# The second batch's attention in float32, with transposes on TensorE and the division after the product

## The chip, the core and the metric

The kernel runs on one core of a Trainium2 chip. The metric is the time on the device of one execution, in microseconds, and lower is better. A core has five engines that each take their instructions in a fixed order: TensorE (PE, products; its weight loads are listed as PEld), VectorE (DVE), ScalarE (ACT), GpSimd (POOL) and SyncE (SP, which here only issues DMAs). Work is handed between them by semaphores. Products are written to PSUM, which has eight banks; everything else lives in SBUF.

## The reference

Attention with a sliding window of 128 and a linear bias over 8 batches, 8 heads, 576 positions and 64 channels, and then a bilinear feed-forward layer over the joined heads:

```python
scores = np.matmul(q, k.transpose(0, 1, 3, 2)) / np.sqrt(D)
mask = (rel >= 0) & (rel < 128)
scores = np.where(mask, scores + bias[None], -1000000000.0)
attn = np.exp(scores - np.max(scores, axis=-1, keepdims=True))
attn = attn / (np.sum(attn, axis=-1, keepdims=True) + 1e-09)
x = np.matmul(attn, v)                 # joined to (B * S, H * D)
out = ((x @ w_a) * (x @ w_b)) @ w_out  # 512 -> 1536 -> 512
```

## The kernel before

The work of a batch is attention for four pairs of heads, then an up projection (twelve blocks `f` of 128 hidden rows, for `w_a` and `w_b`), the product of the two halves, and a down projection. Batches follow each other, and attention of batch b + 1 is woven into the projections of batch b, in sevenths of a pair (`yield i + k / 7`). Float32 precision in the projections comes from splitting each operand into a float16 high and low part and adding three products.

The first batch has no projections to hide behind. Its attention (`first_attention`, L524) works in float32: scores (L569), exponentials without a division (L581), transposes as products with an identity on TensorE (L587), copies of these from PSUM (L592 to L595), the product with v (L501), and then a product of x with the reciprocals of the sums (L619), which an outer product has spread over the channels first (L603 to L614). Beside it run the first steps of `weights`, which loads the projection matrices, converts them from 64-bit words and splits them (L126 to L232). The rest of these steps runs along the first batch's up and down projections (`first_batch`, L999).

All later batches take their attention from `attention` (L658). It already gives the second batch (`o.b == 1`) float32 scores (L374), but then treats it as the others: exponentials (L383), division (`normalize`, L387: the reciprocals, then a float16 high part on ScalarE, L399, and the rest on VectorE, L400, both into the tile `phl`), a DMA transpose of `phl` into `pT` (L405), a split of v into high and low (`split_v`, L291), 42 float16 products a pair (`pv`, L503) and a copy of x (L414).

The first batch's up projection (`first_up`, L776) makes 576 products in groups of twelve, one PSUM bank each. Five banks (three `ef`, two `ch`, by `bank`, L59) go round in turn. A group for `w_a` is read by ScalarE (L783), a group for `w_b` by VectorE (L785), which multiplies the two; a bank is free again when it has been read. The down projection (`first_down`, L804) follows. In this part only SyncE's order is written by hand; a scheduler sets the order on the other engines. From the second batch's projections on, TensorE's order is that of the code.

Of the kernel before, what the change touches and what calls it, by code (L numbers as in the profile page):

```python
# [23 lines left out]
P = 128  # L24
# [5 lines left out]
VCOLS = 640  # L30
# [16 lines left out]
def attention_then_bilinear_ffn(ctx: ExitStack, tc: tile.TileContext, qT, kT, vP, w_a, w_b, w_out, rel, slopes2, outT):  # L47
# [42 lines left out]
    ratio = const.tile([P, NF], F32, name="ratio")  # L90
    smin = const.tile([P, 1], F32, name="smin")
    so = const.tile([P, 1], F32, name="so")

# [110 lines left out]
    def down_weights():  # L204

        sums = small.tile([P, NF // 2], F32, tag="wos", name="wos", bufs=1)
        for n in range(NF // 2 + 1):
# [12 lines left out]
        vec.reciprocal(sab, sab)  # L220
        s1 = small.tile([P, 1], F32, tag="wo1", name="wo1", bufs=1)
        vec.tensor_reduce(out=s1, in_=sums, op=ALU.add, axis=AX)
        tot = ps_at.tile([P, 512], F32, tag="at", name="wtot")
# [134 lines left out]
    def before_scores(o, ninv):  # L358
        o.bias = work.tile([P, WIN], F32, tag="bias", name="bias")
        last_bias[0] = pool.tensor_scalar(out=o.bias, in0=rel_sb, scalar1=ninv, scalar2=sl2_sb[:, o.p:o.p + 1], op0=ALU.mult, op1=ALU.mult)  # L360
        o.mn, o.sm, o.rin = (small.tile([P, 9], F32, tag=tag, name=tag) for tag in ("mn", "sm", "rin"))
        o.n, o.parts = 0, []

    def scores(o, bi):

        ps = ps_at.tile([P, 512], F32, tag="at", name="sc_ps")
        t = work.tile([P, 512], F32, tag="t", name="t", bufs=4)
        for i, c in BANKS[bi]:
# [10 lines left out]
        for i, c in BANKS[bi]:  # L379
            pc, w = TILES[i]  # L380
            n = o.n
            vec.tensor_tensor_reduce(out=t[:, c:c + w], in0=ps[:, c:c + w], in1=o.bias[:, WIN - w:WIN], scale=-0.125 if o.b == 1 else o.neg, scalar=3.0e38, op0=ALU.add, op1=ALU.min, accum_out=o.mn[:, n:n + 1])  # L382
            act.activation(t[:, c:c + w], t[:, c:c + w], AF.Exp, bias=o.mn[:, n:n + 1], scale=-1.0, accum_out=o.sm[:, n:n + 1])  # L383
            o.parts.append((n, t[:, c:c + w], pc, w))
            o.n += 1

    def normalize(o):  # L387

        a, z = o.parts[0][0], o.n

        if o.b < 2:
            vec.tensor_scalar(out=o.rin[:, a:z], in0=o.sm[:, a:z], scalar1=1e-9, scalar2=1.0 / PSC, op0=ALU.add, op1=ALU.mult)
        else:

            act.activation(o.rin[:, a:z], o.sm[:, a:z], AF.Copy, scale=1.0 / PSC, bias=1e-9 / PSC)
        vec.reciprocal(o.rin[:, a:z], o.rin[:, a:z])
        for m, e, pc, w in o.parts:
            s = o.rin[:, m:m + 1]
            act.activation(phl[:, 0, pc:pc + w], e, AF.Copy, scale=s)  # L399
            vec.scalar_tensor_tensor(out=phl[:, 1, pc:pc + w], in0=e, scalar=s, in1=phl[:, 0, pc:pc + w], op0=ALU.mult, op1=ALU.subtract)  # L400
        o.parts = []
# [256 lines left out]
    def attention():  # L658
# [28 lines left out]
        load(0)  # L687
        st, prev = load_v(1), None
        o = squares(0)
        lay_out(o)  # L690
        load(1)
        yield 0
        for i in range(n + 1):
            b, p = 1 + i // NPAIR, i % NPAIR

            two = 2 if o and o.b >= 2 else 1
            for bi in range(two if o else 0):
# [11 lines left out]
            if p == 2:  # L709
# [3 lines left out]
            elif prev and p != 1:  # L713
                prev.vhl = split_v(st, prev.p)
            yield i + 2 / 7
            if p == 2:
                pv(late.p, st, late, late.vhl)
                transpose_probs(prev)
                split(nxt)
            if o and p != 2:  # L720
                with behind():
                    normalize(o)
            if p != 2:
                split(nxt)
            yield i + 3 / 7
            if o:
                scores(o, 2)
            if prev and p not in (1, 2):
                pv(prev.p, st, prev, prev.vhl)
# [5 lines left out]
            yield i + 4 / 7  # L735
            if p == 2:
                prev.vhl = split_v(st, prev.p)
# [6 lines left out]
            load(i + 2)  # L744
            if p == 1:
                v_squares(st, (0, 1))
# [6 lines left out]
            if o:  # L753
                with behind():
                    normalize(o)
            if p == 1:
# [4 lines left out]
            if p == 2:  # L761
                pv(prev.p, st, prev, prev.vhl)
            if p == 1:
                late = prev
# [4 lines left out]

    states, started, first_reads, last_read, last_main, last_bias = {}, {"down": -1}, [None], [None], [None], [None]  # L770


# [202 lines left out]
    first = stack.enter_context(tc.tile_pool(name="first", bufs=1))  # L975
    ident = first.tile([P, P], F32, name="ident")
    make_identity(nc, ident)

# [80 lines left out]
```

## Time and profile before

| | us |
|---|---|
| median of 3 runs | 1007.48 |
| lowest and highest run | 1007.32, 1007.81 |
| span of the profiled execution | 1005.2 |
| first up-projection product of the second batch | 215.10 |

The span goes from the first to the last instruction of one profiled execution. For that execution the profile states the span alone; the median of the runs is 2.3 us above it, and so the time of the profiled execution is taken as its span and those 2.3 us. In the profile a line gives an engine, an operation, and the tiles written and read (out<-in). "Busy" is the time in which an engine executes, and an idle time is put down to what ended it. A float32 product leaves two records in the trace, a transpose one.

### The profile page before, as it was taken

The numbers are of one execution on the slowest core, as the hardware profiler recorded it, in microseconds if no ns is written. First come the engines' busy times: TensorE is split into PE (matmuls) and PEld (weight loads), VectorE is DVE, ScalarE is ACT, GpSimd is POOL, SyncE is SP. The second block draws the span as 40 slices with busy tenths as digits, with TensorE's granted clock in tenths as the row PEclk, the third lists the DMA queues.
The fourth block names the chain that finished last, engine by engine and source line by source line (L and its number), as shares of the span: only waits on it lengthen the run. The fifth ranks groups of instructions, "written<-read, shape, count | busy, mean of one in ns | idle before, by whom it ended". The sixth has DMA issues, their size and how long they took to land.

```text
span 1005.2 us, 23888 instructions
## 1 busy us (share of the span) xinstructions
PE 970.8 (97%) x9339; PEld 753.6 (75%) x9339; DVE 674.8 (67%) x1833; ACT 648.9 (65%) x1715; POOL 306.1 (30%) x345
## 2 busy tenths in 40 slices
PE   8789989999999999999999999999999999999998
PEld 5557656777777777777787777777777777777776
DVE  5888999557878566785768687666677576524530
ACT  7976779657767756767767767677666766413321
POOL 3533463104565321352226112220223022211100
PEclk9889999999999999999999999999999999999999
DMA  9317733564444442462624642474425632210001
GB/s 349 120 43 269 231 114 74 120 166 80 100 90 100 137 90 43 97 172 71 121 52 105 172 90 46 93 178 103 84 57 107 163 67 43 49 37 7 2 13 36
DMA packets 148433, 102.83 MB, mean 102 GB/s; under 512 B 120032, under 2 KB 128352, under 8 KB 147296
## 3 DMA queue, kind: packets, MB, share of 16 engines
q1 hardware_dynamic: 138816, 91.77, 37.2%
q10 hardware_dynamic: 9504, 9.54, 2.9%
q8 instruction: 73, 1.20, 0.5%
q14 instruction: 40, 0.33, 0.1%
HBM read 48.33 MB, written 9.44 MB: 57 GB/s over the span
## 4 chain that ended last, share of the span: by engine, by line
PE 70%; DVE 10%; ACT 4%; DMA 2%; issue 1%; POOL 1%; SPq 0%; ACTq 0%; DVEq 0%
PE dn_ps L932 19%; PE ch L836 19%; PE p L836 14%; PE up_ps L836 10%; PE x_ps L501 4%; PE sc_ps L378 3%; DVE phl L400 2%; PE dn_ps L812 2%; DMA v<-in_vP 1%; DVE t L382 1%; DVE xs L436 1%; ACT t L383 1%; DVE wup L150 1%; ACT phl L399 1%; DVE wup L257 1%
## 5 line engine op out<-in xcount | busy, mean ns | idle before, releaser
L836 PEld LDWEIGHTS <-wup 128*128 128x128 f16 x4224 | 409.1, 98 | 120.8 <-issue 14.3
L932 PE MATMUL dn_ps<-h,wdn 128*128 128x288 f16 x2016 | 254.3, 286 | 0.0
L932 PEld LDWEIGHTS <-wdn 128*128 128x128 f16 x2016 | 193.9, 98 | 51.7
L836 PE MATMUL ch<-xs,wup 128*128 128x288 f16 x1536 | 221.5, 286 | 0.8 <-ACT rc L861 0.6
L836 PE MATMUL up_ps<-xs,wup 128*128 128x288 f16 x1536 | 197.7, 288 | 5.8 <-DVE rc L785 4.2
L836 PE MATMUL p<-xs,wup 128*128 128x288 f16 x1152 | 172.6, 286 | 0.0
L891 POOL TENSOR_TENSOR rc<-rc,row 128x288 f32<-128x288 f32 x64 | 62.3, 974 | 278.8 <-DVE row L889 262.9
L400 DVE SCALAR_TENSOR_TENSOR phl<-t,rin,phl 128x192 f16<-128x192 f32 (+2 forms) x252 | 109.5, 474 | 19.0 <-ACT phl L399 18.8
L383 ACT ACTIVATE t<-t,mn 128x192 f32<-128x192 f32 (+2 forms) x252 | 107.2, 427 | 23.3 <-DVE mn L382 23.0
L829 ACT CAST h<-rc 128x576 f16<-128x576 f32 x96 | 64.2, 669 | 68.2 <-DVE rc L896 37.6
L399 ACT ACTIVATE phl<-t,rin 128x192 f16<-128x192 f32 (+2 forms) x252 | 88.7, 425 | 23.0 <-DMA pT<-phl 10.9
L830 DVE TENSOR_TENSOR h<-rc,h 128x576 f16<-128x576 f32 x90 | 71.1, 790 | 32.7 <-ACT h L829 32.0
L382 DVE CUSTOM_DVE_ANT_0 t<-sc_ps,bias,neg 128x192 f32<-128x192 f32 (+2 forms) x216 | 73.7, 389 | 7.8 <-PE sc_ps L378 7.7
L135 POOL TENSOR_TENSOR wup<-wup,wdn 128x512 int32<-128x512 int32 x36 | 54.6, 1539 | 44.6 <-DVE wup L133 14.6
L937 ACT ACTIVATE row<-dn_ps,oi 128x288 f32<-128x288 f32 x56 | 27.6, 494 | 56.7 <-PE dn_ps L932 56.5
L873 ACT ACTIVATE row<-ch,g 128x288 f32<-128x288 f32 x64 | 31.8, 497 | 50.1 <-PE ch L836 50.1
L436 DVE TENSOR_TENSOR xs<-v,xs 128x576 f16<-128x576 f32 x52 | 48.7, 950 | 21.7 <-ACT xs L435 21.5
L360 POOL TENSOR_SCALAR bias<-rel_sb,ninv,sl_sb 128x192 f32<-128x192 f32 x24 | 21.3, 887 | 123.5 <-DVE mn L382 123.5
L868 DVE TENSOR_TENSOR rc<-p,rc 128x288 f32<-128x288 f32 x64 | 29.1, 454 | 44.4 <-PE p L836 35.0
L896 DVE SCALAR_TENSOR_TENSOR rc<-rc,g,ch 128x288 f32<-128x288 f32 x64 | 32.6, 510 | 23.8 <-PE ch L836 23.6
L383 ACT ACTIVATION_READ_ACCUMULATOR t<-t,mn 128x1 f32 x252 | 47.7, 189 | 0.0
L430 POOL TENSOR_TENSOR xq<-xq,sq 128x576 bf16<-128x576 bf16 x22 | 29.6, 1345 | 56.8 <-ACT sq L429 56.7
(151 smaller groups left out, 1315.6 us busy)
## 6 DMA issues: line engine op xcount, KB each, us to landing
v<-in_vP SPq DMA_DIRECT2D x8, 1280.0 KB, 6.5
out<-row ACTq DMA_DIRECT2D x60, 144.0 KB, 1.8
qk<-in_qT SPq DMA_DIRECT2D x28, 288.0 KB, 3.9
qk<-in_kT SPq DMA_DIRECT2D x28, 288.0 KB, 4.4
wdn<-in_w_a SPq DMA_DIRECT2D x12, 512.0 KB, 4.5
wdn<-in_w_b SPq DMA_DIRECT2D x12, 512.0 KB, 5.6
wdn<-in_w_out SPq DMA_DIRECT2D x12, 512.0 KB, 4.3
qst<-qkh SPq DMA_DIRECT2D x24, 144.0 KB, 2.7
```

Of the source, the lines that this page charges most:

```text
L135: pool.tensor_tensor(out=t[:, m, :], in0=t[:, m, :], in1=low[:, m, :], op=ALU.add)
L382: vec.tensor_tensor_reduce(out=t[:, c:c + w], in0=ps[:, c:c + w], in1=o.bias[:, WIN - w:WIN], scale=-0.125 if o.b == 1 else o.neg, scalar= ...
L383: act.activation(t[:, c:c + w], t[:, c:c + w], AF.Exp, bias=o.mn[:, n:n + 1], scale=-1.0, accum_out=o.sm[:, n:n + 1])
L399: act.activation(phl[:, 0, pc:pc + w], e, AF.Copy, scale=s)
L400: vec.scalar_tensor_tensor(out=phl[:, 1, pc:pc + w], in0=e, scalar=s, in1=phl[:, 0, pc:pc + w], op0=ALU.mult, op1=ALU.subtract)
L436: vec.tensor_tensor(out=xs[:, n, 1, :, :], in0=src, in1=xs[:, n, 0, :, :], op=ALU.subtract)
L501: pe.matmul(xp[oc // 512][64 * h:64 * h + 64, o0:o0 + w], vt[0:rows, c:c + 64], probs(pt, rows, blocks, h), start=(n == 0 and first), stop ...
L829: act.copy(h[:, f, :, 0, :], hid)
L830: eng.tensor_tensor(out=h[:, f, :, 1, :], in0=hid, in1=h[:, f, :, 0, :], op=ALU.subtract)
L836: pe.matmul(ps[:, 0:HT], wup[:, a[0], a[1], wi, k, :], xs[:, b, xi, k, :], start=(first and n == 0), stop=(last and n == len(ks) - 1), ski ...
L891: pool.tensor_tensor(out=x0, in0=x0, in1=mid, op=ALU.mult)
L932: pe.matmul(ps[:, 0:HT], wdn[:, f, wi, e * P:(e + 1) * P], h[:, f, t, hi, :], start=(m == 0 and n == 0), stop=(m == NF - 1 and n == 2))
```

## The change

The second batch takes the first batch's way. Its exponentials stay undivided in four fixed buffers (`plain_ts`), zeroed once where the window leaves gaps. They are transposed on TensorE with the identity, copied from PSUM into a float32 tile (`phl` for even pairs, `pT` for odd ones), multiplied with v in float32, and x is multiplied with the spread reciprocals and v's scale on VectorE (`plain_pv`, which runs one pair behind in four steps). The splits of v and of the probabilities, the DMA transposes and the copy of x fall away for this batch. v's sums of squares and scale move to an earlier place; `phl` is zeroed when the third batch begins instead of before the projections. The identity stays allocated, and a few small tiles are merged.

```diff
+    two_scales = const.tile([P, 2], F32, name="two_scales")
+    smin, so = two_scales[:, 0:1], two_scales[:, 1:2]
+    ident = const.tile([P, P], F32, name="ident")
+    make_identity(nc, ident)
...
     def before_scores(o, ninv):
...
+        if o.b == 1:
+            o.pT = (new_pT().rearrange("p a c -> p (a c)") if o.p % 2 else phl.rearrange("p a c -> p (a c)")).bitcast(F32).rearrange("p (b q) -> p b q", q=P)
...
-        t = work.tile([P, 512], F32, tag="t", name="t", bufs=4)
+        t = plain_ts[bi] if o.b == 1 else work.tile([P, 512], F32, tag="t", name="t", bufs=4)
...
-            o.parts.append((n, t[:, c:c + w], pc, w))
+            o.parts.append((n, t[:, c:c + w], pc, w) if o.b > 1 else (bi, t))
...
+    def transpose_plain(o):
+        for bi, t in dict(o.parts).items():
+            tp = bank("tr_ps")
+            for k in range(4):
+                pe.transpose(tp[:, 128 * k:128 * k + 128], t[:, 128 * k:128 * k + 128], ident)
+            if bi == 0:
+                act.copy(o.pT[:, 0:2, :], tp[:, 0:256].rearrange("k (b q) -> k b q", q=P))
+                act.copy(o.pT[:, 14:16, :], tp[:, 256:512].rearrange("k (b q) -> k b q", q=P))
+            else:
+                (vec.tensor_copy if bi % 2 else act.copy)(o.pT[:, 4 * bi - 2:4 * bi + 2, :], tp.rearrange("k (b q) -> k b q", q=P))
+        o.parts = []
+
+    def plain_pv(p, st, o):
+        rin = o.rin
+        vec.tensor_scalar(out=rin, in0=o.sm, scalar1=1e-9, scalar2=None, op0=ALU.add)
+        vec.reciprocal(rin, rin)
+        yield
+        rp = [bank("rin_ps") for _ in range(2)]
+        order = [n for b in range(4) for n, _ in BANKS[b]]
+        for n, i in enumerate(order):
+            for e in range(2):
+                r = slice(64 * e, 64 * e + 64)
+                pe.matmul(rp[i // 8][r, 64 * (i % 8):64 * (i % 8) + 64], rin[r, n:n + 1].to_broadcast([64, 64]), ident[r, r], start=True, stop=True)
+        r = work.tile([P, 2, VCOLS], F16, tag="vhl", name="rinv", bufs=2).rearrange("p a c -> p (a c)").bitcast(F32)
+        x = st.v[:, p, 0:S]
+        parts = ((0, 512), (512, 64))
+        for n, (c, w) in enumerate(parts):
+            act.copy(r[:, c:c + w], rp[n][:, 0:w])
+        yield
+        xp = new_x_ps()
+        each_pv(xp, (st.v[:, p, :],), (o.pT,))
+        yield
+        for n, (c, w) in enumerate(parts):
+            vec.scalar_tensor_tensor(out=x[:, c:c + w], in0=xp[n][:, 0:w], scalar=st.sv, in1=r[:, c:c + w], op0=ALU.mult, op1=ALU.mult)
+        square_x(p, st, x)
+        yield
+
     def normalize(o):
+        if o.b == 1:
+            return transpose_plain(o)
...
+        plain_ts[:] = [work.tile([P, 512], F32, tag="t", name="t", bufs=4) for _ in range(4)]
+        for bi, t in enumerate(plain_ts):
+            for c, w in ((64, 64), (448, 64)) if bi == 0 else ((192, 128),):
+                pool.memset(t[:, c:c + w], 0.0)
...
+            behind_it = plain_pv(prev.p, st, prev) if prev and prev.b == 1 else iter(())
+            if i == NPAIR:
+                for c, w in ((64, 64), (448, 128), (960, 128), (1472, 128), (1984, 64)):
+                    pool.memset(phl[:, :, c:c + w], 0.0)
...
-            if p == 2:
+            if p == 2 and b > 1 or i == 1:
                 v_scale(st)
+            next(behind_it, None)
...
-            if p == 1:
+            if p == 1 and b > 1 or i == 0:
                 v_squares(st, (0, 1))
...
-    for c, w in ((64, 64), (448, 128), (960, 128), (1472, 128), (1984, 64)):
-        pool.memset(phl[:, :, c:c + w], 0.0)
```

The order of the instructions shows what moves. Line numbers of the changed program differ: there L895 are the up projection's products (before L836), L871 the down projection's (L812), L378 the second batch's scores (L374), L844 VectorE's product behind the up projection (L785), L233 the down weights' low parts (L231), L396 the new transposes, L415 the new spread of the reciprocals and L542 the product with v (L501).

On TensorE, beside the up projection, there stood only scores among the projection's products (before):

```order
L836 LDWEIGHTS wup
L836 MATMUL up_ps<-xs,wup 128x288
L374 MATMUL sc_ps<-qkl,qkh 64x192 x4
L836 LDWEIGHTS wup
L836 MATMUL up_ps<-xs,wup 128x288
```

At such a place in the changed program stand, for the second batch's second pair of heads, scores and transposes of the exponentials:

```order
L378 MATMUL sc_ps<-qkl,qkh 64x192 x3
L895 LDWEIGHTS wup
L895 MATMUL up_ps<-xs,wup 128x288
L895 LDWEIGHTS wup
L895 MATMUL up_ps<-xs,wup 128x288
L396 MATMUL tr_ps<-ident,t 128x128 x2
L895 LDWEIGHTS wup
L895 MATMUL up_ps<-xs,wup 128x288
L895 LDWEIGHTS wup
L895 MATMUL up_ps<-xs,wup 128x288
L396 MATMUL tr_ps<-ident,t 128x128 x2
```

Two transposes, which wait for ScalarE's exponentials, have come between projection products, and the four together fill one of the five banks that the projection uses.

On TensorE, beside the down projection, the changed program has for the third and fourth pair:

```order
L871 MATMUL dn_ps<-h,wdn 128x288
L378 MATMUL sc_ps<-qkl,qkh 64x192 x2
L542 MATMUL x_ps<-phl,v 64x128
L396 MATMUL tr_ps<-ident,t 128x128 x4
L542 MATMUL x_ps<-phl,v 64x128 x3
L542 MATMUL x_ps<-phl,v 64x256 x4
L542 MATMUL x_ps<-phl,v 64x128 x2
L542 MATMUL x_ps<-phl,v 64x64 x4
```

The 14 float32 products with v stand where 42 float16 ones, each with a weight load of its own, stood before.

On VectorE, beside the up projection, the splits of the probabilities (L400) stood between the weights' conversions (L131, L133) and the product that frees a bank (before):

```order
L400 SCALAR_TENSOR_TENSOR phl<-t,rin,phl 128x192
L113 TENSOR_SCALAR r<-cl 128x1
L400 SCALAR_TENSOR_TENSOR phl<-t,rin,phl 128x192 x2
L114 TENSOR_SCALAR sv<-r 128x1
L131 TENSOR_SCALAR wup<-wdn 128x2x512
L400 SCALAR_TENSOR_TENSOR phl<-t,rin,phl 128x192
L131 TENSOR_SCALAR wup<-wdn 128x2x512
L785 SCALAR_TENSOR_TENSOR rc<-rc,g,up_ps 128x288
L133 SCALAR_TENSOR_TENSOR wup<-wdn,wup 128x2x512 x2
```

Near the end of the up projection the changed program has the down weights' low parts between two such products (the second one comes after more of the same):

```order
L233 SCALAR_TENSOR_TENSOR wdn<-wup,ratio,wdn 128x512
L844 SCALAR_TENSOR_TENSOR rc<-rc,g,up_ps 128x288
L233 SCALAR_TENSOR_TENSOR wdn<-wup,ratio,wdn 128x512 x2
L386 ISA t,mn<-sc_ps,bias 128x192
L386 ISA mn 128x1
L386 ISA t,mn<-sc_ps,bias 128x192
L386 ISA mn 128x1
L233 SCALAR_TENSOR_TENSOR wdn<-wup,ratio,wdn 128x512 x6
```

The splits of the probabilities are gone, and the run of L233 (L231 before) has come nearer to the front against the up projection's products.

More of the change, by code (lines that the diff above doesn't have):

```diff
@@ L204, in down_weights @@
     def down_weights():
-        sums = small.tile([P, NF // 2], F32, tag="wos", name="wos", bufs=1)
+        sums = small.tile([P, NF // 2 + 1], F32, tag="wos", name="wos", bufs=1)
         for n in range(NF // 2 + 1):
@@ L220, in down_weights @@
         vec.reciprocal(sab, sab)
-        s1 = small.tile([P, 1], F32, tag="wo1", name="wo1", bufs=1)
-        vec.tensor_reduce(out=s1, in_=sums, op=ALU.add, axis=AX)
+        s1 = sums[:, NF // 2:NF // 2 + 1]
+        vec.tensor_reduce(out=s1, in_=sums[:, 0:NF // 2], op=ALU.add, axis=AX)
         tot = ps_at.tile([P, 512], F32, tag="at", name="wtot")
@@ L727, in attention @@
                 scores(o, 2)
-            if prev and p not in (1, 2):
+            next(behind_it, None)
+            if prev and p not in (1, 2) and prev.b > 1:
                 pv(prev.p, st, prev, prev.vhl)
```

35 lines of the change are left out of this document (18 added, 17 removed).

## The prediction

> **What bounds the kernel now.** I read the page first. Its rows say how long the execution took, how busy each engine was, and, in 40 slices, how busy TensorE and VectorE were and which clock TensorE was granted.
>
> ```profile
> span 1005.2 us, 23888 instructions
> PE 970.8 (97%) x9339; PEld 753.6 (75%) x9339; DVE 674.8 (67%) x1833; ACT 648.9 (65%) x1715; POOL 306.1 (30%) x345
> ...
> PE   8789989999999999999999999999999999999998
> ...
> DVE  5888999557878566785768687666677576524530
> ...
> PEclk9889999999999999999999999999999999999999
> ```
>
> TensorE is busy for 97% of the span, so it is the bound, and only work that it gains or waits that it loses can move the end. The clock row shows the only throttled slices at the front. The change touches the second batch's attention, which runs beside the first batch's up and down projections. I therefore cut the span there: the columns are the length of a stretch, then busy us of PE, PEld, DVE, ACT and POOL, then the granted clock.
>
> ```profile
> 71.50:100.00 28.50, 28.36 (x237) 21.49 (x235) 25.37 (x48) 20.20 (x43) 9.41 (x10) 0.99 0.62 233
> 100.00:125.00 25.00, 22.80 (x178) 16.68 (x176) 23.97 (x48) 18.52 (x41) 11.43 (x13) 0.93 0.74 236
> 125.00:150.00 25.00, 20.79 (x192) 14.64 (x191) 24.49 (x43) 19.02 (x44) 16.71 (x11) 0.93 0.35 110
> 150.00:169.50 19.50, 17.32 (x176) 12.78 (x173) 17.82 (x51) 18.77 (x43) 5.81 (x5) 1.00 0.28 58
> 169.50:215.10 45.60, 44.09 (x450) 33.58 (x449) 28.34 (x97) 29.29 (x89) 8.49 (x7) 1.00 0.64 135
> 215.10:1005.20 790.10, 781.47 (x7538) 614.59 (x7537) 501.02 (x1406) 485.76 (x1310) 220.85 (x248) 1.00 0.37 85
> ```
>
> The first batch's up projection runs to 169.5 us and its down projection to 215.1 us. Up to 71.5 us TensorE's instructions stand in the same order in both programs, so I count nothing before. From 100 to 169.5 us it is idle 25 - 22.80, 25 - 20.79 and 19.5 - 17.32 us, 8.6 us together, while VectorE has 66.28 of 69.5 us filled (95%): that stretch is VectorE's as much as TensorE's. The waits of TensorE in this stage say the same:
>
> ```profile
> PE up_ps L836 <- DVE rc L785: 4.2, 2, 2.3
> PE wtot L101 <- ACT t L383: 1.7, 1, 1.7
> PE wn_ps L156 <- ACT wdn L141: 1.5, 1, 1.5
> PE n_ps L515 <- ACT row L822: 1.1, 1, 1.1
> PE sc_ps L374 <- DVE mn L382: 0.7, 1, 0.7
> PE up_ps L836 <- ACT rc L783: 0.5, 1, 0.5
> ```
>
> The largest is for L785, VectorE's product that frees an up-projection PSUM bank. The n_ps wait of 1.1 us lies at the end of the down projection and is not touched. After the two long waits the clock is halved for one piece each:
>
> ```profile
> 103.00:106.40 3.40, 3.21 (x16) 1.99 (x17) 2.41 (x7) 1.96 (x8) 1.64 (x3) 0.52 0.92 237
> 133.70:137.10 3.40, 3.29 (x16) 1.91 (x17) 3.40 (x16) 3.40 (x13) 1.28 (x1) 0.52 0.56 218
> ```
>
> At 0.52 and 0.52, these 3.4 us pieces lose 1.6 us each, 3.3 us together. So what the change could at most win back here is 8.6 + 3.3 = **11.9 us**.
>
> **The change part by part: TensorE.** For each of four pairs of heads it adds 16 float32 transposes and 18 small float32 products that spread the reciprocals, and it replaces 42 float16 products of probabilities and values by 14 in float32. All three kinds stand in the first batch's attention in this trace, so they have rows. The columns are start, time, line and operation; the next row's start gives the price in a stream.
>
> ```profile
> 46.03 0.60 PE L587 MATMUL tr_ps<-ident,t 128*128 128x128 f32 x4
> 46.56 0.86 PE L569 MATMUL sc_ps<-qk 64*64 64x192 f32 x6
> ...
> 50.20 1.15 PE L610 MATMUL rin_ps<-ident,rin 64*64 64x64 f32 x32
> 51.18 0.82 PE L569 MATMUL sc_ps<-qk 64*64 64x192 f32 x8
> ...
> 55.24 2.12 PE L501 MATMUL x_ps<-phl,v 128*64 128x128 f32 x28
> 57.29 0.44 PE L587 MATMUL tr_ps<-ident,t 128*128 128x128 f32 x2
> ...
> 58.30 0.38 PE L587 MATMUL tr_ps<-ident,t 128*128 128x128 f32 x2
> 58.52 0.90 PE L836 MATMUL up_ps<-xs,wup 128*128 128x288 f16 x6
> ...
> 159.58 1.65 PE L501 MATMUL x_ps<-pT,vhl 128*64 128x128 f16 x42
> 161.16 3.11 PE L836 MATMUL up_ps<-xs,wup 128*128 128x288 f16 x24
> ```
>
> - Transposes: 4 take 46.56 - 46.03 = 0.53 us, so 16 take 2.12 us. From below, 2 take 58.52 - 58.30 = 0.22, so 1.76 us; from above, four groups at the full 0.60 are 2.4 us.
> - Reciprocals: in float32 each product leaves two records, so x32 is 16 products in 51.18 - 50.20 = 0.98 us, and 18 take 1.10 us. From above 18/16 of 1.15 is 1.29 us.
> - Products with x: 57.29 - 55.24 = 2.05 us in float32 against 161.16 - 159.58 = 1.58 us in float16, so +0.47 us a pair, little changed from above (2.12 - 1.58 = 0.54).
>
> A pair adds 2.12 + 1.10 + 0.47 = 3.69 us, four pairs **14.8 us**; the bounds are 4 x (1.76 + 1.10 + 0.47) = 13.3 us and 4 x (2.4 + 1.29 + 0.54) = 16.9 us. I take the middle, as groups of four are the commonest form in the new order. This is in TensorE's own stream, so nothing hides it: it can only fill time in which TensorE waits today.
>
> **VectorE and ScalarE.** The hi/lo splitting of probabilities (L399, L400) and of v (L295, L296) goes for this batch; copies of the transposes (the form of L595) and the product with the reciprocals (the form of L619) come.
>
> ```profile
> L400 DVE SCALAR_TENSOR_TENSOR phl<-t,rin,phl 128x192 f16<-128x192 f32 (+2 forms) x36 | 16.1, 491 | 0.6 <-ACT phl L399 0.5
> L399 ACT ACTIVATE phl<-t,rin 128x192 f16<-128x192 f32 (+2 forms) x36 | 12.6, 424 | 1.2 <-DVE rin L396 1.2
> L296 DVE SCALAR_TENSOR_TENSOR vhl<-v,sv,vhl 128x640 f16<-128x640 f32 x4 | 6.6, 1661 | 1.5 <-ACT vhl L295 1.5
> L295 ACT ACTIVATE vhl<-v,sv 128x640 f16<-128x640 f32 x4 | 3.2, 813 | 0.0
> ...
> L595 DVE COPY pT<-tr_ps 128x512 f32<-128x512 f32 x4 | 2.7, 682 | 0.6 <-PE tr_ps L587 0.6
> L619 DVE SCALAR_TENSOR_TENSOR v<-x_ps,sv,rin 128x512 f32<-128x512 f32 x4 | 3.0, 748 | 4.7 <-PE x_ps L501 4.6
> ```
>
> VectorE loses 16.1 + 6.6 = 22.7 us and gains 8 copies x 0.682 = 5.5 us and 4 x 0.748 = 3.0 us, a net 14 us less (the narrow parts and the instructions on nine sums per row are left out on both sides). About three of the four pairs lie in the up projection, so some 10 us of VectorE leave the 98 us after 71.5 us: 25.37 + 66.28 - 10 = 82 us, 84% instead of 94%. ScalarE loses 12.6 + 3.2 us and gets copies back. The first 28.5 us at 89% of VectorE cost TensorE only 0.14 us; the 69.5 us at 95% cost it 12%. By the nearest row, then, most of the wait goes. Not all of it: every engine takes its instructions in a fixed order, the new transposes and reciprocal products need the same five rotating PSUM banks as the up projection and wait for ScalarE's exponentials and VectorE's reciprocals themselves, and behind them on TensorE stand up-projection products. I keep **4 us** of the 11.9 (bounds 0 and 11.9), which is 4% of the stretch, between the 0.5% at the 89% row and the 12% at the 95% row.
>
> **SyncE, GpSimd and PSUM.** Four DMA transposes of probabilities leave SP's queue. No TensorE wait above names a DMA, so I count this as nothing; nothing is late behind it. GpSimd's zeroing of phl moves from the front to the start of the third batch's attention, and four small buffers are zeroed instead; GpSimd is busy for 30% of the span and TensorE's waits name no line of it, so its own idle time hides them and I count nothing; without that cover a fill would cost its own length, a small part of the smallest wait above.
>
> **The sum.** 14.8 added, 11.9 - 4 = 7.9 won back: +6.9 us on the execution's span of 1005.2 us. Between span and the median of 1007.48 us lie 2.3 us, which I leave as they are: 1005.2 + 6.9 + 2.3 = 1014.4, and I say **1014 us**. A change under 0.2% (2 us) could not be told from none here. The terms' bounds give 13.3 - 11.9 = +1.4 to 16.9 us, so 1009 to 1024 us.
>
> **The rivals.**
>
> - *VectorE stays the limit* (waits move instead of going): the added 14.8 us come on top of the old waits, 1022 us; half of it 1018. For it: the new order puts a run of weight splits between two bank-freeing products of VectorE, and VectorE's share was 95%. Against it: 22.7 us of its work are gone, 8.5 come.
> - *The clock drops.* The halved pieces above cost 1.6 us each. If the transposes left TensorE's activity too low, one such piece per pair would come, 4 x 1.6 = 6.4 us, so 1021 us. Against it: at 46.03 and 58.30 us groups of transposes stand among other products, and none of them or the products behind them runs at half speed. The Trainium skill, "TensorE: Matmul & The Clock Gate", Part 4: PE-mode transpose, states that a transpose does not count as busy time for the clock gate in the way that a product does. By that rule the halved pieces would come; the rows of this trace do not show it, since no group here is longer than a few transposes.
> - *All waits vanish and the adds are cheap*: +1.4 to +2 us, within 0.2%.
> - *Faster.* The 64x64 and 128x64 float32 products use a part of the array. If they ran beside the neighbouring float16 products, the 14.8 us would shrink. Under 9.9 us, that is under 2.5 us a pair, with all 11.9 us won back, the kernel would be faster by 2 us; at half the price, 7.4 - 11.9 = -4.5 us, 1003 us. Against it: the two transposes at 58.30 us delayed the up products behind them by their whole 0.22 us, and the product groups in the trace start only as the ones ahead end.
>
> **How the numbers follow.** My forecast (1010 to 1017.5 us) has 0.55; VectorE staying the limit 0.14; the clock 0.06; no change 0.17; faster 0.08. Faster by over 0.2% is 0.08, within 0.2% 0.17, slower 0.75. The range from 1007 to 1021 us takes in the forecast, the lower half of the two slow rivals and most of the no-change case, and leaves out about 0.2; the bound of 1024 needs the top price and every old wait at once.
>
> **What would show it.** If I am right, TensorE's busy time from 71.5 us to the second batch's up projection grows by 13 to 17 us, its idle time there falls from about 10 us to 5 or less, the waits for L785's successor shrink, VectorE's busy time falls by about 13 us, and the stretch after it keeps its length. Idle time still near 10 us means the first rival; more half-clock pieces the second; busy time growing by under 10 us the last. The forecast falls if the stretch behind 215.1 us changes its length by more than 2 us, as I have costed it at nothing.

## The result and the profile after

The changed kernel takes 1022.87 us (median of 4 runs, 1020.45 to 1023.13), the kernel before beside it 1007.64 us (1007.32 to 1008.81). The ratio is 1.0146, 95% interval 1.0134 to 1.0158: 15.2 us slower where the prediction had about 7. The profiled execution took 1022.62 us. The page of the changed kernel, in the same three kinds of row as before:

```profile
span 1020.8 us, 24127 instructions
...
PE 987.6 (97%) x9491; PEld 767.8 (75%) x9491; DVE 661.1 (65%) x1801; ACT 639.5 (63%) x1687; POOL 303.6 (30%) x350
...
PEclk7799999999999999999999999999999999999999
```

TensorE has 16.8 us more to do, the span is 15.6 us longer, and VectorE has 13.7 us less to do, as forecast. The time is found by cutting the span where TensorE goes from one stage to the next: its first long run of up products, its first down product, and the second batch's first up product. In the view by windows the first number of a row is the length; then come busy us of PE, PEld, DVE, ACT and POOL, and the clock. Before:

```profile
71.53:169.54 98.01, 89.28 (x775) 65.63 (x774) 91.66 (x188) 76.52 (x170) 43.36 (x36) 0.96 0.52 167
169.54:215.10 45.56, 44.05 (x450) 33.54 (x449) 28.30 (x97) 29.25 (x89) 8.49 (x7) 1.00 0.64 135
```

After:

```profile
73.52:178.08 104.56, 98.44 (x907) 74.09 (x906) 86.64 (x183) 77.16 (x171) 43.65 (x38) 1.00 0.39 140
178.08:228.89 50.81, 48.81 (x470) 37.29 (x468) 20.08 (x77) 21.11 (x63) 6.01 (x10) 1.00 0.34 78
228.89:1020.80 791.91, 782.86 (x7538) 615.25 (x7537) 500.39 (x1402) 485.51 (x1310) 220.37 (x248) 1.00 0.37 85
```

The 15.6 us are 2.0 ahead of the up projection (73.5 - 71.5), 6.55 in it, 5.25 in the down projection and 1.8 behind (791.91 - 790.10). In the two projections, before, TensorE worked 89.28 + 44.05 - 3.3 (the halved clock) = 130.0 us; after, 98.44 + 48.81 = 147.25 us: **17.2 us of work came**. What it lost to waits and the halved clock was 8.73 + 1.51 + 3.3 = 13.5 us and is 6.12 + 2.00 = 8.1 us: **5.4 us were won back**, and 17.2 - 5.4 is the 11.8 us of the two stages.

The work is close to its terms. With the next row's start as the end, as in the prediction, the 64 transposes take 8.1 us (forecast 8.5), the 72 spread products 5.3 (4.4), the products with v 8.9 against 6.3 (+2.6, forecast +1.9). The other 1.2 us lie in the up products and scores, which now stand in shorter runs; that the shorter runs cost it is not shown. Some rows of the changed timeline:

```profile
141.92 1.21 PE L415 MATMUL rin_ps<-ident,rin 64*64 64x64 f32 x36
143.07 1.64 PE L895 MATMUL up_ps<-xs,wup 128*128 128x288 f16 x12
...
147.84 1.07 PE L396 MATMUL tr_ps<-ident,t 128*128 128x128 f32 x8
148.75 1.63 PE L895 MATMUL up_ps<-xs,wup 128*128 128x288 f16 x12
...
228.89 2.86 PE L895 MATMUL up_ps<-xs,wup 128*128 128x288 f16 x12 [2.00 <-DVE row L879]
```

Eighteen spread products take 143.07 - 141.92 = 1.15 us (forecast 1.10), eight transposes 0.91 us, 0.114 each (forecast 0.13). The last row is the stage's end: 2.00 us of waiting for VectorE, and twelve products that take 2.86 us where twelve take 1.63 elsewhere. TensorE's waits in the changed up projection are many and small, and no longer for one line:

```profile
PE up_ps L895 <- ACT phl L401: 1.3, 1, 1.3
PE tr_ps L396 <- ACT t L387: 1.2, 2, 0.7
PE up_ps L895 <- ACT rc L842: 1.1, 2, 0.7
PE wn_ps L158 <- DVE wtop L163: 0.9, 1, 0.9
```

The transposes wait for exponentials (L387), and an up group waits for the copy that frees a bank from transposes (L401).

### The profile page after: what moved, and what is told of

It is laid out like the page before. It is cut to its first block, busy times and chain, and to the rows that moved or that the text cites. A ratio compares the mean times of both kernels' runs of the same rounds, so it can differ in the third digit from the quotient of the medians.

```text
span 1020.8 us, 24127 instructions
## 1 busy us (share of the span) xinstructions
PE 987.6 (97%) x9491; PEld 767.8 (75%) x9491; DVE 661.1 (65%) x1801; ACT 639.5 (63%) x1687; POOL 303.6 (30%) x350
## 4 chain that ended last, share of the span: by engine, by line
PE 70%; DVE 7%; ACT 6%; DMA 3%; issue 1%; POOL 1%; ACTq 0%; SPq 0%; DVEq 0%
PE ch L895 18%; PE dn_ps L991 17%; PE p L895 13%; PE up_ps L895 11%; PE x_ps L542 4%; PE dn_ps L871 4%; PE sc_ps L382 3%; DVE phl L441 1%; DMA v<-in_vP 1%; DVE xs L477 1%; DVE wup L259 1%; ACT t L387 1%; DVE t L386 1%; DMA wdn<-in_w_out 1%; ACT wdn L232 1%
## 5 line engine op out<-in xcount | busy, mean ns | idle before, releaser
L895 PEld LDWEIGHTS <-wup 128*128 128x128 f16 x4224 | 408.9, 98 | 118.2 <-issue 12.3
L895 PE MATMUL ch<-xs,wup 128*128 128x288 f16 x1536 | 221.5, 286 | 1.8 <-ACT rc L920 1.2
L895 PE MATMUL up_ps<-xs,wup 128*128 128x288 f16 x1536 | 198.0, 287 | 5.1 <-DVE row L879 2.0
L895 PE MATMUL p<-xs,wup 128*128 128x288 f16 x1152 | 172.6, 286 | 0.0
L387 ACT ACTIVATE t<-t,mn 128x192 f32<-128x192 f32 (+2 forms) x252 | 107.2, 427 | 36.4 <-DVE mn L386 36.2
L441 DVE SCALAR_TENSOR_TENSOR phl<-t,rin,phl 128x192 f16<-128x192 f32 (+2 forms) x216 | 92.7, 470 | 13.6 <-ACT phl L440 13.4
L440 ACT ACTIVATE phl<-t,rin 128x192 f16<-128x192 f32 (+2 forms) x216 | 76.2, 425 | 17.8 <-DVE rin L437 8.2
L476 ACT CAST xs<-v 128x576 f16<-128x576 f32 x52 | 34.1, 667 | 22.2 <-POOL v L495 8.4
```

Of the source, the lines that this page charges most:

```text
L895: pe.matmul(ps[:, 0:HT], wup[:, a[0], a[1], wi, k, :], xs[:, b, xi, k, :], start=(first and n == 0), stop=(last and n == len(ks) - 1), ski ...
```

## The experiments

Besides the changed kernel's work, two things are open: whether VectorE's relief wins anything back, and what the up projection waits for. Up and dn are the lengths of the stages cut as above, in each profiled execution (T0 is the up projection's start, rest what follows the down projection); the kernel before had medians of 1007.65 to 1008.18 us beside them.

| kernel | T0 | up | dn | rest | median us | ratio to before, 95% |
|---|---|---|---|---|---|---|
| before | 71.5 | 98.0 | 45.6 | 790.1 | 1007.64 | |
| after | 73.5 | 104.6 | 50.8 | 791.9 | 1022.87 | 1.0146 [1.0134, 1.0158] |
| after_again | 72.5 | 104.1 | 50.9 | 791.5 | 1020.73 | 1.0130 [1.0114, 1.0146] |
| no_spread | 73.3 | 100.6 | 47.8 | 789.8 | 1011.90 | 1.0043 [1.0030, 1.0055] |
| half_tr | 72.2 | 99.6 | 48.6 | 792.0 | 1014.08 | 1.0062 [1.0050, 1.0075] |
| filler | 72.0 | 105.2 | 50.8 | 790.0 | 1019.56 | 1.0121 [1.0105, 1.0136] |
| relief | 71.8 | 98.4 | 46.0 | 789.3 | 1009.12 | 1.0010 [1.0000, 1.0020] |
| adds | 72.6 | 101.3 | 48.7 | 789.8 | 1013.25 | 1.0053 [1.0041, 1.0065] |
| front_edits | 74.0 | 96.2 | 46.3 | 790.8 | 1006.88 | 0.9987 [0.9975, 0.9999] |
| adds_relief | 73.3 | 105.1 | 49.0 | 789.3 | 1017.41 | 1.0090 [1.0075, 1.0105] |
| ident_in | 73.2 | 100.3 | 50.9 | 790.4 | 1016.38 | 1.0078 [1.0065, 1.0092] |
| no_copies | 72.9 | 105.8 | 51.4 | 790.1 | 1019.13 | 1.0109 [1.0095, 1.0124] |
| relief_chain | 70.5 | 94.8 | 45.1 | 790.6 | 1003.14 | 0.9947 [0.9934, 0.9959] |
| before_chain | 69.9 | 91.0 | 48.4 | 791.6 | 1001.00 | 0.9932 [0.9919, 0.9945] |
| after_chain | 68.8 | 105.5 | 50.9 | 792.5 | 1019.23 | 1.0112 [1.0098, 1.0127] |
| before_or | 68.5 | 92.4 | 52.7 | 790.9 | 1005.90 | 0.9980 [0.9972, 0.9989] |

### Parts of the change taken away

The changed kernel once more, as the base for these:

> The changed kernel unaltered, as the base for the three beside it and for how the front varies. If the later start of the projections is luck of an execution, its runs spread over 1020 to 1023 us; if it belongs to the kernel, nearly all lie at 1022.5 to 1023.2 us.

1020.73 us (1019.37 to 1022.95). So the changed kernel has a spread of 3.6 us of its own, and the other kernels are held against this run. The traces show one thing more that all comparisons below have to bear: every edit but filler's gave another order of instructions on TensorE, VectorE and ScalarE, so the other kernels do not differ from their base in the edit alone.

The spread of the reciprocals away:

```diff
-        rp = [bank("rin_ps") for _ in range(2)]
...
-                pe.matmul(rp[i // 8][r, 64 * (i % 8):64 * (i % 8) + 64], rin[r, n:n + 1].to_broadcast([64, 64]), ident[r, r], start=True, stop=True)
...
-            act.copy(r[:, c:c + w], rp[n][:, 0:w])
...
-            vec.scalar_tensor_tensor(out=x[:, c:c + w], in0=xp[n][:, 0:w], scalar=st.sv, in1=r[:, c:c + w], op0=ALU.mult, op1=ALU.mult)
+            vec.tensor_scalar(out=x[:, c:c + w], in0=xp[n][:, 0:w], scalar1=st.sv, scalar2=None, op0=ALU.mult)
```

> The changed kernel without the outer products that spread the reciprocals (18 products a pair), without their copies, and without the reciprocals as a factor of x, so the second batch's x is not divided by its sums. Price of the products by their row: 4 x 1.10 = 4.4 us less than the changed kernel, 1018.4 us. If they lie in TensorE's waits, under 2 us less. If they cost their two PSUM banks and ScalarE copies as well, 6 us or more less.

8.8 us less. TensorE's busy time in the two stages falls by (98.37 + 48.81) - (95.33 + 45.85) = 6.0 us, and the rest is 1.7 us shorter: the piece at halved clock behind the boundary is gone. Without that piece it is 7.1 us, still more than the 5.3 us of stream.

The transposes and copies of pairs 2 and 3 away:

```diff
     def transpose_plain(o):
+        if o.p >= 2:
+            o.parts = []
+            return
```

> The changed kernel without the transposes and their copies for the third and fourth pair of the second batch, which use the transposed exponentials of the first and second pair. Those lie at the end of the up projection and in the down projection, where TensorE hardly waits. By the row 32 transposes x 0.133 us = 4.2 us less, 1018.6 us. If the breaks that each group makes cost extra, 5 us or more less. If they lie in waits, under 3 us less.

6.65 us less, by 6.0 us of TensorE's busy time: 32 transposes are 4.0 us of stream, and most of the other 2 us lie in the scores, the spread products and the products with v, which take less time in this order. Taken away, the spread and half of the transposes (with their copies) are each worth more than their time in the stream.

Thirty small products ahead of the second batch's first up product, to fill the wait for VectorE there:

```diff
+        fill = ps_at.tile([P, 512], F32, tag="at", name="fill_ps")
+        for n in range(30):
+            pe.matmul(fill[:, 0:P], ones16, ones16, start=True, stop=True)
```

> The changed kernel with 30 products of 128 columns put between the first batch's down projection and the second batch's up projection, in a bank of their own, read by nobody, where TensorE waits 2.0 us in the profile of the changed kernel and the clock is halved for 3.4 us after it. If the halved clock comes from that wait, 1.6 us less than the changed kernel, 1021.2 us, and no halved piece after the boundary. If not, the same time, or up to 0.5 us more.

The first 3.4 us of the last stage, in the changed kernel and then with the filler:

```profile
228.90:232.30 3.40, 3.40 (x17) 2.19 (x17) 1.33 (x8) 1.66 (x7) 0.00 (x0) 0.53 0.92 283
```

```profile
228.05:231.45 3.40, 3.40 (x29) 2.73 (x29) 1.09 (x5) 1.26 (x6) 0.00 (x0) 1.00 0.96 296
```

The granted clock, the third number from the end, goes from 0.53 to 1.00, and the stretch behind is 1.5 us shorter (790.05 against 791.53 in after_again); the medians differ by 1.2 us, within their spreads. So most of the 1.8 us behind the boundary are a clock that halves after the 2.0 us wait.

### The two sides of the change apart, on the kernel before

VectorE's part of the split taken away, and nothing added:

```diff
             act.activation(phl[:, 0, pc:pc + w], e, AF.Copy, scale=s)
-            vec.scalar_tensor_tensor(out=phl[:, 1, pc:pc + w], in0=e, scalar=s, in1=phl[:, 0, pc:pc + w], op0=ALU.mult, op1=ALU.subtract)
+            if o.b > 1:
+                vec.scalar_tensor_tensor(out=phl[:, 1, pc:pc + w], in0=e, scalar=s, in1=phl[:, 0, pc:pc + w], op0=ALU.mult, op1=ALU.subtract)
```

> The kernel before, without VectorE's low parts of the second batch's probabilities (36 instructions, 16.1 us of VectorE); the low half of phl is zeroed once, so the second batch's output lacks the low parts. TensorE's own work is as before. The forecast's theory (VectorE's load is what TensorE waits for in the first batch's up projection): of 11.9 us of waits and halved clock 6 to 8 us go, 1000 to 1002 us. Rival (the waits are made by the fixed order and move to other instructions when VectorE is relieved): 3 us or less go, 1004.5 to 1007.6 us.

The up projection by windows, and TensorE's waits in it:

```profile
71.81:170.24 98.43, 87.94 (x773) 65.00 (x773) 83.59 (x166) 77.87 (x172) 44.36 (x36) 0.98 0.52 167
```

```profile
PE up_ps L837 <- DVE rc L786: 4.3, 1, 4.3
PE wn_ps L156 <- ACT wdn L141: 3.8, 3, 2.3
PE up_ps L837 <- ACT rc L784: 1.9, 2, 1.1
```

VectorE lost 8 us, from 94% to 85% of the stage, and the stage is as long as before; TensorE's idle time in it is 98.43 - 87.94 = 10.5 us, up from 8.7. The wait for VectorE's L786 (L785 before) is as large as it was, and the one for the converted weights (L141) has grown. The median is 1.2 us above the kernel before, outside both cases of the expectation. This run speaks against the step on VectorE's share.

TensorE's new work added with nothing taken away: 8 transposes of the identity and 9 spread products in each `normalize` of the second batch, into the same banks, read by nobody (the early identity and the merged small tiles of the change are in it too):

```diff
+        if o.b == 1:
+            for _ in range(2):
+                tp = bank("tr_ps")
+                for k in range(4):
+                    pe.transpose(tp[:, 128 * k:128 * k + 128], ident, ident)
+            rp = bank("rin_ps")
+            for n in range(9):
+                r = slice(64 * (n % 2), 64 * (n % 2) + 64)
+                pe.matmul(rp[r, 64 * (n // 2):64 * (n // 2) + 64], ident[r, n:n + 1].to_broadcast([64, 64]), ident[r, r], start=True, stop=True)
```

> The kernel before, with 16 transposes of the identity and 18 small float32 products with it for each of the second batch's four pairs, in banks of the projections' rotation, read by nobody: TensorE's additions without the relief. Price by the rows of before: 4 x (2.12 + 1.10) = 12.9 us, 1020.5 us if nothing of it falls into TensorE's waits. If the additions fill the old waits of 8.6 us, 1013 to 1016 us. If the additions cost more in a stream than their rows (a break of the projection's products at each group), over 1022 us.

```profile
72.58:173.85 101.27, 98.17 (x931) 74.23 (x929) 90.20 (x193) 80.34 (x181) 48.08 (x38) 0.98 0.54 166
```

Only 5.3 us more than before (0.53% of 1008 us), though TensorE has 98.17 - 89.28 = 8.9 us more busy time in this stage alone. Its idle time fell to 101.27 - 98.17 = 3.1 us with VectorE at 89% and every split still there. Work that waits for no result of the stage (its largest wait for a bank is 1.2 us) fills the old waits by itself.

The identity allocated early, the merged small tiles and the zeroed buffers alone:

> The kernel before, with the change's edits ahead of the projections alone: the identity kept in the constants, the merged small tiles, the four buffers zeroed at the same place (and used by nobody there). If the 2.0 us by which the changed kernel reaches the up projection later come from these edits: 1009.6 us. If they come from how the clock and the first loads fell in that execution: 1007.6 us, within 0.5 us.

1006.88 us: as a whole these cost nothing. Their own trace, however, starts the up projection late too, at 74.0 us, and has it 1.8 us shorter, so it does not part a cost ahead of that stage from a gain in it. Where GpSimd keeps its additions, T0 lies between 71.5 and 74.0 us, and between 72.0 and 73.5 us in the changed kernel and its variants; so the 2.0 us are not put down to the change. (The four kernels further down with fewer additions on GpSimd have 68.5 to 70.5 us.)

Both together, the additions and the relief:

> The kernel with TensorE's additions (read by nobody), and in it also without VectorE's low parts of the second batch's probabilities. Additions alone gave 1013.3 us, the relief alone 1009.1. If VectorE's load still costs anything once TensorE is fuller, 1011.5 us or less, and the 3.1 us of idle time that were left in the up projection go. If TensorE's own added work had already filled all that could be filled, 1012.8 to 1013.8 us.

A miss: 1017.41 us, slower than the additions alone, with an up projection of 105.1 us against 101.3. With less work on VectorE the scheduler wrote another order, TensorE is idle for 7.5 us in it instead of 3.1, and its waits are these:

```profile
PE wtot L103 <- ACT v L426: 2.6, 1, 2.6
PE tr_ps L409 <- ACT rc L795: 2.2, 2, 2.0
PE up_ps L848 <- DVE rc L797: 1.5, 1, 1.5
```

### What the remaining waits in the changed kernel are for

The same transposes, of the identity in place of the exponentials, so that they wait for no exponential:

```diff
-                pe.transpose(tp[:, 128 * k:128 * k + 128], t[:, 128 * k:128 * k + 128], ident)
+                pe.transpose(tp[:, 128 * k:128 * k + 128], ident, ident)
```

> The changed kernel, but its transposes read the identity instead of the exponentials, so they wait for no exponential, and the second batch's product with v is of identities; the copies stay. If the new waits of TensorE come from ScalarE's exponentials: 6.1 us of idle time in the up projection fall to about 4, up and down projection 153 us instead of 155.2, 1018.7 us. If they come from the banks and their copies, unchanged, 155 us and 1020.7 us.

1016.38 us, 4.35 us less than after_again and below both cases of the expectation; the up projection takes 100.3 us. The waits of `tr_ps` for L387 and of `up_ps` for the copies (L401) are gone from the list. But of the 3.8 us by which this stage is shorter than in after_again only 1.4 are idle time (5.8 to 4.4 us); the others are TensorE's busy time, 98.37 to 95.95 us. The order changes with the edit too, so the 4.35 us belong to both.

All transposes, but no copies from PSUM for pairs 2 and 3:

```diff
+            if o.p >= 2:
+                continue
             if bi == 0:
                 act.copy(o.pT[:, 0:2, :], tp[:, 0:256].rearrange("k (b q) -> k b q", q=P))
```

> The changed kernel with all transposes, but without the copies from PSUM for the third and fourth pair, which use the copied transposes of the first and second. Beside the run without these 32 transposes and their copies (up and down projection 148.2 us) and the changed kernel (155.2 us): the transposes' own price is 32 x 0.127 = 4.1 us. If only that counts, 152.3 us and 1018 us, and the copies and their banks cost the other 3 us; if the copies cost nothing, 155 us and 1020.7 us.

A miss: 1019.13 us, inside the spread of the changed kernel, and up 105.8 us. No price of the copies shows here.

### The waits of the kernel before

Before the up products can use a weight block, its words go from VectorE (L131, L133) through an integer addition on GpSimd (L135) to ScalarE (L141) and then to TensorE's norms (L156). ScalarE's own largest wait in the up projection before, and GpSimd's additions there:

```profile
ACT wdn L141 <- POOL wup L135: 10.6, 7, 2.3
```

```profile
L135 POOL TENSOR_TENSOR wup<-wup,wdn 128x512 int32<-128x512 int32 x20 | 31.1, 1579 | 27.1 <-DVE wup L133 9.6 <-ACT wdn L130 8.1 <-ACT vhl L295 4.2
```

Two additions of 1.58 us stand one behind the other for each block. The next three kernels move the second of them to VectorE from the sixth block on, so that the two can run side by side; the first also has relief's edit:

```diff
         for m in range(2):
-            pool.tensor_tensor(out=t[:, m, :], in0=t[:, m, :], in1=low[:, m, :], op=ALU.add)
+            (vec if m and n >= 5 else pool).tensor_tensor(out=t[:, m, :], in0=t[:, m, :], in1=low[:, m, :], op=ALU.add)
```

> The kernel before without VectorE's low parts of the second batch's probabilities, and with the second half of each addition in the weights' conversion (L135) on VectorE instead of GpSimd from the sixth matrix pair on (its rounding differs). The relief alone left 10.4 us of idle time in the up projection, and ScalarE waited for these additions. If the weights' chain from GpSimd through ScalarE to TensorE is what TensorE waits for there: 4 us or more less, 1004 us or less. If the waits lie elsewhere: 1007 to 1010 us.

1003.14 us, 6 us below relief, as the first case expected.

> The kernel before with one edit: from the sixth matrix pair on the second half of each addition in the weights' conversion (L135) on VectorE instead of GpSimd; nothing is left out. With VectorE also relieved of the low parts this gave 1003.1 us. If the weights' chain alone is what TensorE waits for: 1002.5 to 1004.5 us here too. If VectorE, 94% full in this stretch, can only carry it when relieved: 1006 us or more.

The one edit on the kernel before, with nothing left out, takes **1001.00 us** (998.74 to 1002.68), ratio 0.9932: faster than both kernels of this document and below the range expected, and relief's edit adds nothing to it.

```profile
69.86:160.81 90.95, 86.42 (x768) 64.65 (x766) 85.25 (x193) 74.82 (x169) 28.48 (x26) 0.98 0.57 180
```

```profile
L135 DVE CUSTOM_DVE_ANT_0 wup<-wdn,wup 128x1024 uint16<-128x1024 uint16 x10 | 8.3, 825 | 0.0
```

VectorE got 8.3 us *more* to do and has 94% of a stage that is 7 us shorter. It runs the addition on 16-bit parts; the expectation's remark on rounding is not shown. The down projection gives 2.9 us back.

Yet VectorE's busy time in the stage fell, from 91.66 to 85.25 us, mostly because its other instructions became shorter (three splits of the down weights also moved to the next stage). The largest group, before and in this run:

```profile
L150 DVE SCALAR_TENSOR_TENSOR wup<-wup,sup 128x512 f16<-128x512 f32 x13 | 15.4, 1205 | 1.0 <-ACT wup L149 1.0
```

```profile
L150 DVE SCALAR_TENSOR_TENSOR wup<-wup,sup 128x512 f16<-128x512 f32 x13 | 9.4, 747 | 0.0
```

What goes with the longer ones stands in the timeline before, ahead of TensorE's longest wait for L785 (rows of VectorE, GpSimd and TensorE, in order of time):

```profile
129.12 2.44 DVE L150 SCALAR_TENSOR_TENSOR wup<-wup,sup 128x512 f16<-128x512 f32 x2
129.34 3.36 POOL L135 TENSOR_TENSOR wup<-wup,wdn 128x512 int32<-128x512 int32 x2 [2.14 <-ACT wdn L141]
...
131.63 1.63 DVE L150 SCALAR_TENSOR_TENSOR wup<-wup,sup 128x512 f16<-128x512 f32 x1
...
133.25 0.50 DVE L785 SCALAR_TENSOR_TENSOR rc<-rc,g,up_ps 128x288 f32<-128x288 f32 x1
...
133.81 3.04 PE L836 MATMUL up_ps<-xs,wup 128*128 128x288 f16 x12 [2.31 <-DVE rc L785]
```

The three of these 13 L150 with no GpSimd instruction beside them take 0.74 to 0.75 us; beside GpSimd's additions they take up to 1.78 us. In this stage of the kernel before, 20 of VectorE's instructions took over 0.12 us more than the short time of their own form, 19 us together, and each of the 20 overlaps an instruction of GpSimd; in before_chain there are 12 such, with 9.5 us. L785, which reads PSUM, takes 0.50 us either way. So a fifth of VectorE's 91.66 us was this lengthening beside GpSimd, and the edit that takes additions from GpSimd came with shorter VectorE instructions as well as a shorter chain. In relief, too, the wait of 4.3 us follows three L150 and a split of the hidden rows (1.83 us, 0.75 us where GpSimd rests) beside two of GpSimd's additions; taking the probabilities' low parts from VectorE left these alone.

> The changed kernel with the same edit of L135. Its VectorE has room (86.6 of 104.6 us in the up projection). If the 6.1 us of idle time that it keeps there are waits for the weights' chain: 4 us or more less, 1016.5 us or less. If they are waits that its own transposes and reciprocals bring (for exponentials and for banks): 2 us less at most, 1018.5 to 1020.7 us.

1019.23 us, 1.5 us below after_again, within the spread and in the second case of the expectation; the up projection is no shorter (105.5 us).

```profile
PE up_ps L895 <- DVE rc L844: 3.3, 2, 2.1
PE up_ps L895 <- ACT phl L401: 1.1, 1, 1.1
```

What the edit wins before, the changed kernel does not win: TensorE's idle time in the stage is 6.3 us (6.1 without the edit), and its largest wait is now for VectorE's product (L844). Why is not shown; it is not the second case's reason alone, which named exponentials and banks.

In the last kernel ScalarE converts half of such a block, and VectorE joins the other half by a shift and an or:

```diff
-        act.activation(low, low.bitcast(U32), AF.Copy, scale=float(2.0**-29))
+        k = 1 if n >= 5 else 2
+        act.activation(low[:, 0:k, :], low[:, 0:k, :].bitcast(U32), AF.Copy, scale=float(2.0**-29))
...
+        if k == 1:
+            vec.scalar_tensor_tensor(out=t[:, 1, :], in0=low[:, 1, :], scalar=29, in1=t[:, 1, :], op0=ALU.logical_shift_right, op1=ALU.bitwise_or)
+        for m in range(k):
```

> The kernel before, from the sixth matrix pair on with the second half of the low bits joined by one shift-and-or on VectorE in place of ScalarE's conversion and GpSimd's addition (it cuts the low bits off instead of rounding them). Shorter chain than by VectorE's addition of 1.14 us. If the length of the chain counts: 1003 us or less. If VectorE's load counts: 1006 us or more.

1005.90 us, between the two cases of the expectation. The up projection is nearly as short (92.4 us), but the down projection takes 52.7 us, with this wait in it:

```profile
PE x_ps L504 <- DMA pT<-phl: 4.3, 2, 2.7
```

Much of the gain came back as a wait for the DMA transposes of probabilities, one stage later.

## Why the prediction was right in direction and wrong in size

The kernel is slower for the reason named, work on TensorE's own stream, but by twice the sum.

- **Added work**, 14.8 us forecast with bounds of 13.3 and 16.9: 17.2 us, just above the bound. The three terms came to 8.1 + 5.3 + 2.6 = 16.0 us; the 1.2 us in the up products and scores were no term at all.
- **The step that failed: "By the nearest row, then, most of the wait goes", and from it the 4 us kept of 11.9.** It took VectorE's share of 95% for the measure of TensorE's waits. Relief took VectorE to 85%, and TensorE's idle time rose to 10.5 us in a stage of 98.4 us. In two more pairs, too, the kernel with less of this work on VectorE was not faster: adds_relief beside adds (1017.41 and 1013.25 us), relief_chain beside before_chain (1003.14 and 1001.00 us). The stage is shorter in all three kernels on this base that take additions from GpSimd, which the prediction had set aside because TensorE's waits name no line of it: by 7.1 us in before_chain, 3.7 in relief_chain beside relief, 5.6 in before_or. TensorE's waits name ScalarE's L141, whose own wait names GpSimd, and VectorE's L785, behind instructions that are longer beside GpSimd; one step further back in the trace shows both. Which of the two made the gain, the shorter chain or the shorter VectorE instructions, the runs do not part, nor the share of the new order: front_edits, which takes no work away, has the stage 1.8 us shorter as well. The Trainium skill, "Perfetto Trace Analysis", Identifying the Most-Contended Engine, says to find the bottleneck by occupancy (for TensorE by other measures, the share of its weight loads among them) and to work on the fullest engine first; in this stage VectorE had 94% and TensorE's weight loads 67%, and taking 8 us from VectorE gave nothing, so here the rule did not lead to what helped.
- **Won back**, 7.9 us forecast: 5.4. The halved clock (3.3 us) did go, and idle time in the up projection fell from 8.7 to 6.1 us, not to 5 or less. Adds shows that added work can fill those waits without any relief: additions alone left 3.1 us idle.
- **The stretch behind**, costed at nothing: 1.8 us in the profiled execution, and the 2 us bound on it nearly reached. Nearly all of it is one piece at 0.53 of the clock, behind the boundary's wait of 2.0 us (the wait itself counts to the down projection). The prediction had said that the boundary's wait of 1.1 us is not touched.
- **The front**, costed at nothing: 2.0 us in this execution; by front_edits' median the edits there cost nothing as a whole, and its own T0 is later still, so what the 2.0 us come from stays open.
- From 6.9 to 15.6 us of span there are thus 2.4 us more work, 2.5 us less won back, 1.8 us behind and 2.0 us ahead of the stages.
- **The rivals.** "VectorE stays the limit" gave the right time, 1022 us, by luck: it kept all of the old waits under 14.8 us of work, while 17.2 us of work came and 5.4 us were won back, and VectorE had 83% of the stage (86.64 of 104.56 us). "The clock drops" fell in the place named: the up projection holds 48 of the transposes, and its clock is 1.00 over all 104.56 us. By the rule of the Trainium skill that the prediction weighed ("TensorE: Matmul & The Clock Gate", Part 4: PE-mode transpose) halved pieces would have come there; in groups of two to eight among products, this trace shows none. In adds one such piece did come (113.4 to 116.8 us at 0.50), behind eight transposes and nine spread products with waits of 0.47 and 1.19 us among them; whether those groups or the waits brought it is not shown.

Adds shows that 8.9 + 3.9 us more of busy TensorE (the second number from the down projection, 47.90 - 44.05) cost 5.3 us, near the sum forecast. The changed kernel lies 7.5 us (after_again) above it. Of that, the products with v are 2.6 us of stream and the boundary with its clock 1.7 (791.5 - 789.8); ident_in puts about 4 us on the dependence on exponentials and the order around it, of which 1.4 us are idle time of the up projection. What stays open: adds_relief has the same long up projection (105.1 us) without any dependence on exponentials, so an unlucky order alone can make as much, and the runs do not part the two. Nor is it shown which of its waits the scheduler could have avoided.

## What to carry to other kernels

A full engine beside a waiting one is no proof that the wait goes when that engine gets less to do. Follow the wait through the engine it names to what that engine waits for, and see whether its instructions take longer there than elsewhere, and beside what; then try the edit at that place. Work added to the engine that bounds a kernel is paid in full except where it can start without waiting; if it depends on results of the same stage it can bring waits of its own, so price these too. Where a scheduler writes the order, an edit that takes work away may cost time, and only running it tells.

## What the runs showed of the hardware

- One wait of 2.00, 2.13 or 2.35 us at the boundary (after, after_again, half_tr) was followed by products at about half speed (twelve in 2.7 to 2.9 us); after 1.90 us (no_spread) twelve took 1.63 us. The length of the wait alone does not decide it: in relief a wait of 2.31 us ends at 112.96 us, and the clock of the next 3.4 us is 1.00. The Trainium skill, "TensorE: Matmul & The Clock Gate", Part 1, speaks of a free-running window of about 3.4 us; the halved pieces here last one such length, yet they follow waits that are shorter than it.
- VectorE's instructions on SBUF alone can take about 1 us longer beside GpSimd's: the 128x512 split of the weights (L150) 0.74 us alone and up to 1.78 us beside them, in the up projection of the kernel before; L785, which reads PSUM, 0.50 us with and without.
- VectorE adds the 128x512 integers in 0.83 us in before_chain, GpSimd in 1.34 to 1.65 us (before_chain to before_or). The same form on VectorE took 1.33 us in the changed kernel with this edit:

```profile
L137 DVE CUSTOM_DVE_ANT_0 wup<-wdn,wup 128x1024 uint16<-128x1024 uint16 x10 | 13.2, 1326 | 0.0
```

Here all ten overlap an addition of GpSimd and take 0.68 to 1.79 us; in before_chain the three with GpSimd at rest take 0.68 us each, the others up to 1.63 us.
